# Two half-height products side by side in TensorE's array, in a fused linear-attention and SwiGLU kernel

## The chip, the cores and the metric

The kernel runs on one core of a Trainium2 chip. A core has TensorE (PE; its weight loads are shown as PEld), VectorE (DVE), ScalarE (ACT), GpSimd (POOL) and SyncE (SP, which here issues the DMAs). The metric is the device time of one execution in microseconds (us); lower is better. Of the kernel before there are three timed runs and one profiled execution.

## The reference

For 2048 tokens of 640 features two branches are computed from the same x and mixed by a gate of each token:

```
g   = sigmoid(sum(x * gate_w))
q, k, v = x @ wqkv                       # 32 heads of 20
phi(y)  = concat(softmax(y @ w_phi), softmax(-(y @ w_phi)))
a   = (phi(q) @ (phi(k)^T v)) / (phi(q) . sum(phi(k)) + 1e-6) @ wo
b   = (silu(x @ w_gate) * (x @ w_up)) @ w_down
out = g * a + (1 - g) * b
```

The inner size of the second branch (the feed-forward part) is F = 1728 = 13 x 128 + 64. Inputs and output are bf16.

## The kernel before, in words

Tokens are taken in 16 tiles of 128, or in 4 blocks (`bt`) of 512. Everything that TensorE multiplies lies in SBUF; all products go to PSUM, which is used as 8 banks of 512 f32 columns, or as 4 pairs of banks where a result has 640 columns.

*Feed-forward.* For a block and each of 14 pieces `k` of F (`ffn`, L620), TensorE makes gate and up (5 matmuls of 512 columns each, as 640 = 5 x 128), into one bank each. `ffn_tail` (L592) turns them into a piece of h: ACT takes tanh of the gate into `hT` and copies up into `us`, DVE makes (tanh + 1) * gate in `hT` (L611), POOL multiplies by `us` (L617). Piece 13 has only 64 features: its gate and up stand side by side as one stationary operand of 128 columns (`wg[:, c, 1664:1792]`, L626 to L628), so that gate comes out in PSUM rows 0 to 63 and up in rows 64 to 127. Its h fills rows 0 to 63 of `hT[:, :, 13, :]`; rows 64 to 127 are set to zero once (L543), as are those of `wd[:, 13, :]` (L544).

*Down.* `down` (L709) takes one token tile: 14 matmuls of 512 columns and 14 of 128 into one pair of banks, each with 128 rows (pieces 0 to 12 full, piece 13 half zeros). The stationary operand is a 128x128 tile of `hT`, the moving one a row block of `wd`. The last tile's two column parts are separate tasks, so that the first can be written out while the second runs.

*Attention.* `features` (L799) makes the k and q features: projection on TensorE, then on DVE max, min (L831, L835), two subtractions (L839, L843), exp on ACT, sum and reciprocal on DVE (L854, L858), the division on POOL (L864). `kvpart` sums phi(k)^T v; `qtile` (L922) transposes phi(q) by DMA, multiplies it (`num`), divides, transposes by DMA and multiplies by `wo`. `finish` and `finals` mix the two branches and store a tile.

*What sets the order.* Nothing is ordered by the chip: a planner (`_Plan`, L229) is given every step as a task with an engine, a cost in us, what it depends on, a priority, and what it takes and gives back (a bank, a pair, a slot of a buffer). It plays the program through once by these costs, and each task's instructions are recorded when the planner starts it. So each engine's queue is fixed when the kernel is built, and semaphores guard it when it runs. `down` asks for one pair. The feed-forward and down tasks have priorities by their place in a list (L982 to L993). The constants at L658 to L666 are due times and intervals for k and q tiles (`K_AT`, `K_EACH`, `Q_AT`, `Q_EACH`), and `D_AFTER` and `K_PAIRS` shape the list. All loads (L516 to L535) go through SP's queue in one chain, in which a landing time is assumed for each. All matmuls have one line, that of the helper `mms` (L434), and all activations that of `actop` (L444); they are told apart by their tiles.

Of the kernel before, what the change touches and what calls it, by code (L numbers as in the profile page):

```python
# [6 lines left out]
P = 128  # L7
# [221 lines left out]
class _Plan:  # L229
# [11 lines left out]
    def add(self, eng, cost, fn, deps=(), prio=5.0, lat=None, acq=(), rel=(), name=""):  # L241
        t = _Task(eng, cost, fn, deps, prio, self.LAT[eng] if lat is None else lat,
                  tuple(acq), tuple(rel), len(self.tasks), name)
        self.tasks.append(t)
        return t
# [82 lines left out]
def _mm(*cols):  # L328
    return sum(c / 2400.0 + 0.003 for c in cols)


def _build(
# [22 lines left out]
    def sb(name, shape, dtype):  # L355
        t = nc.alloc_sbuf_tensor(name, list(shape), dtype)
        tr.reg_tensor(t, "sbuf", nc.lookup_mloc(t).addr, rowelems(shape), mybir.dt.size(dtype))
        return t
# [8 lines left out]
    wvg = sb("wvg", [P, 5, D + 1], BF16)  # L367
    wo = sb("wo", [P, 5, D], BF16)
    wd = sb("wd", [P, NK, D], BF16)
    wg = sb("wg", [P, 5, F_FFN + 64], BF16)  # L370
    wu = sb("wu", [P, 5, 13 * P], BF16)
    hT = sb("hT", [P, 2, NK, 512], BF16)
    us = sb("us", [P, 3, 512], BF16)
# [37 lines left out]
    def bank(i, j, c0, c1, r0=0, r1=P):  # L411
        return ps[r0:r1, (2 * i + j) * 512 + c0:(2 * i + j) * 512 + c1]

    def one(b, c0, c1, r0=0, r1=P):
        return ps[r0:r1, b * 512 + c0:b * 512 + c1]
# [22 lines left out]
    def acc(o, pairs):  # L438
        n = len(pairs)
        return [(o, l, r, i == 0, i == n - 1) for i, (l, r) in enumerate(pairs)]  # L440
# [5 lines left out]
    def dveop(fn, reads, writes):  # L446
        run("dve", fn, reads=reads, writes=writes)

    def poolop(fn, reads, writes):
        run("pool", fn, reads=reads, writes=writes)  # L450

    def memset(t_ap, val, eng):
        eobj = {"pool": pool, "dve": dve}[eng]
        run(eng, lambda: eobj.memset(t_ap, val), reads=[], writes=[t_ap])  # L454
# [18 lines left out]
    def load(eng, dst, src, land, prio, transpose=False, name="load", cost=0.06):  # L473

        t = add(eng, cost, lambda: dma(eng, dst, src, transpose=transpose), prio=prio, lat=2.0, name=name)
        t.land = land
        t.slack = L_SLACK if land > 11 else 0.0
        t.after = chain.get(eng)
        chain[eng] = t
        return t  # L480

    def rows(a):
        return a.rearrange("(c p) j -> p c j", p=P)
# [12 lines left out]
    def load_x(bt, prio, *cuts):  # L496

        tok = slice(512 * bt, 512 * bt + 512)
        out_ = []
        for i, (c0, c1, land) in enumerate(cuts):  # L500
            out_ += [load("sp", xT[:, c0:c1, tok], x2[tok, c0 * P:c1 * P], land, prio + 0.1 * i, True, "x%d" % bt)] * (c1 - c0)
        return out_

    def load_wT(which, land, prio):
        o = 5 * which
        return load("sp", wqT[:, o:o + 5, :], A_wqkv[:, which * D:(which + 1) * D], land, prio, True, "wT")
# [3 lines left out]
    def load_gate():  # L510
        with nc.allow_non_contiguous_dma(reason="gate_w column load (640 elems)"):
# [16 lines left out]
    load_gu(4, "sp", (32.4, 33.9), -30)  # L528
    wgl[NPC] = load("sp", wg[:, :, 1664:1728], gsrc[:, :, 1664:1728], 34.2, -29)
    wul[NPC] = load("sp", wg[:, :, 1728:1792], usrc[:, :, 1664:1728], 34.6, -28)  # L530
    xs[3] = load_x(3, -27, (0, 5, 37.4))
    wqT_l = load_wT(0, 41.5, -26)
    wd_l = [load("sp", wd[:, 0:13, :], rows(B_w_down[0:13 * P, :]), 48.5, -25),
            load("sp", wd[0:64, 13, :], B_w_down[13 * P:F_FFN, :], 49.0, -24)]
    wo_l = load("sp", wo[:, :, :], rows(A_wo), 51.0, -23)  # L535
    xl = [x_[4] for x_ in xs]


# [1 line left out]
    zero = add("dve", 0.3, lambda: memset(us[:, 0, :], 0.0, "dve"), prio=-20, name="zero")  # L540
    table = add("act", 1.3, lambda: actop(us[:, 1, 0:1], us[:, 0, 0:1], ACTF.Tanh), deps=[zero], prio=-20, name="table")
    ones_t = add("dve", 0.4, lambda: memset(v1ones, 1.0, "dve"), prio=-19)
    add("dve", 1.0, lambda: memset(hT[64:P, :, 13, :], 0.0, "dve"), prio=-18)  # L543
    wdz = add("dve", 0.7, lambda: memset(wd[64:P, 13, :], 0.0, "dve"), prio=-18)  # L544
    wd_l[1].deps.append(wdz)

    def build_wbd(c):
        nh = PHI_NH[c]
# [42 lines left out]

    def ffn_tail(bt, k, ctx, last, n_after):  # L592
        hb = bt % 2
        rows = P if k < 13 else 64
        hap = hT[0:rows, hb, k, :]

        def gap():
            return one(ctx["g"], 0, 512, 0, rows)

        def uap():  # L600
            return one(ctx["u"], 0, 512) if k < 13 else one(ctx["g"], 0, 512, 64, P)

        def usa():
            return us[0:rows, ctx["us"], :]
        t1 = add("act", 0.49, lambda: actop(hap, gap(), ACTF.Tanh, scale=0.5), deps=[last[0]], prio=0, name="tanh")
        t2 = add("act", 0.49, lambda: actop(usa(), uap(), ACTF.Copy, scale=0.5), deps=[last[1]], prio=0.1,
                 acq=[("us", ctx, "us")], rel=[("bank", ctx, "u")] if k < 13 else (), name="us")

        def stt():
            g_ = gap()  # L610
            dveop(lambda: dve.scalar_tensor_tensor(out=hap, in0=hap, scalar=1.0, in1=g_, op0=ALU.add, op1=ALU.mult),  # L611
                  [hap, g_], [hap])
        t3 = add("dve", 0.59, stt, deps=[t1, t2] if k == 13 else [t1], prio=0, rel=[("bank", ctx, "g")], name="stt")

        def mult():
            u_ = usa()
            poolop(lambda: pool.tensor_tensor(hap, hap, u_, ALU.mult), [hap, u_], [hap])  # L617
        mult_t[bt, k] = add("pool", 1.11, mult, deps=[t2, t3], prio=0, rel=[("us", ctx, "us")], name="hmul")

    def ffn(bt, k, rank):  # L620
        tsl = slice(512 * bt, 512 * bt + 512)
        ctx = {}
        before = [down_t.get((bt - 2, u)) for u in range(4)]
        w_ = w_dep(k)
        if k == 13:
            gu = add("pe", _mm(*[512] * 5), lambda: mms(acc(one(ctx["g"], 0, 512),  # L626
                      [(wg[:, c, 1664:1792], xT[:, c, tsl]) for c in range(5)])),
                      deps=before + [xl[bt], wgl[NPC], wul[NPC]], prio=rank, acq=[("bank", ctx, "g")], name="gu")  # L628
            ffn_tail(bt, k, ctx, (gu, gu), 0)
            return  # L630
        g_ = add("pe", _mm(*[512] * 5), lambda: mms(acc(one(ctx["g"], 0, 512),
                 [(wg[:, c, P * k:P * k + P], xT[:, c, tsl]) for c in range(5)])),
                 deps=before + [xl[bt], wgl[w_]], prio=rank, acq=[("bank", ctx, "g")], name="gate")
        u_ = add("pe", _mm(*[512] * 5), lambda: mms(acc(one(ctx["u"], 0, 512),
                 [(wu[:, c, P * k:P * k + P], xT[:, c, tsl]) for c in range(5)])),
                 deps=[wul[w_]], prio=0.0, acq=[("bank", ctx, "u")], name="up")
        u_.after = g_
        ffn_tail(bt, k, ctx, (g_, u_), 0)
# [17 lines left out]
            ffn_tail(0, k, cs[k], lasts, 0)  # L656

    B_FIRST = 8  # L658
    K_AT, K_EACH, Q_AT, Q_EACH = 26.0, 5.70, 118.6, 8.46
    PRE_Q = 10.10  # L660
    PRE_EACH = 2.2
    PRE_AT = 21.0
    D_AFTER = 1
    FIN_DVE = 12
    K_PAIRS = 7
    store_t = {}  # L666
    gs_t = {}
    pend = []
# [38 lines left out]
                deps=[f], prio=1, name="out")  # L707

    def down(bt, u, rank):  # L709
        t = 4 * bt + u  # L710
        ctx = {}
        hb = bt % 2
        tk = slice(P * u, P * u + P)

        def part(j):
            return acc(bank(ctx["ps"], j, 0, P if j else 512),
                       [(hT[:, hb, k, tk], wd[:, k, 512:D] if j else wd[:, k, 0:512]) for k in range(NK)])
        hold = {"deps": [mult_t[bt, k] for k in range(NK)] + wd_l, "prio": rank, "acq": [("pair", ctx, "ps")], "name": "down"}
        if t < NT - 1:
            d_ = add("pe", _mm(*([512] * 14 + [128] * 14)), lambda: mms(part(0) + part(1)), **hold)  # L720
            down_t[bt, u] = d_
            return t, ctx, d_
        first = add("pe", _mm(*[512] * 14), lambda: mms(part(0)), **hold)
        second = add("pe", _mm(*[128] * 14), lambda: mms(part(1)), prio=0.0, name="down")
        second.after = first
        down_t[bt, u] = second
        return t, ctx, [(first, 0, 512), (second, 512, D)]

# [252 lines left out]
    seq += [("f", k, 0) for k in range(K_PAIRS, NK)]  # L983
    for bt in range(1, NBT):
        ks = list(range(K_PAIRS if bt == 1 else 0, NK))
        ds = [("d", u, bt - 1) for u in range(4)]
        for i, k in enumerate(ks):
            seq.append(("f", k, bt))
            if i >= D_AFTER and ds:
                seq.append(ds.pop(0))  # L990
        seq += ds
    late = [e for e in seq if e[0] == "d" and e[2] == NBT - 2][2:]
    seq = [e for e in seq if e not in late] + late + [("d", u, NBT - 1) for u in range(4)]  # L993
    downs = []
    for i, (kind, j, bt) in enumerate(seq):
        if kind == "f":
            ffn(bt, j, 10.0 + 0.01 * i)
        else:
            downs.append(down(bt, j, 10.0 + 0.01 * i))
    for t in range(NT):  # L1000
        qtile(t, 5.0 + 0.01 * t)
    for t, ctx, d_ in downs:
# [55 lines left out]
```

## Time and profile before

| what | value |
|---|---|
| median of 3 runs (lowest, highest) | 289.60 us (289.57, 289.64) |
| the profiled execution's own time | 289.35 us |
| its span, first to last instruction | 287.2 us |
| granted TensorE clock | 1.000 |
| POOL, division of the features (L864), 32 times | 77.6 us busy |
| TensorE, gate and up matmuls (`wg`, `wu`), 524 records | 131.8 us busy |
| TensorE, down matmuls (`wd`), 443 records | 62.5 us busy |
| DMA, share of 16 engines in the first 40 us | near 1.0 |

A busy time is the time in which at least one instruction of the row or engine ran. The matmul rows need care: TensorE starts a matmul before the one ahead of it has ended, so a mean duration is longer than the distance between starts, and a count times a mean is more than the busy time. A few matmul records are missing (443 of the 448 of `down` are there). "Idle before" is time in which the engine of a row did nothing, with what ended it.

### The profile page before, as it was taken

What the parts mean: (1) busy time and instruction counts of PE and PEld (TensorE: products, weight loads), DVE (VectorE), ACT (ScalarE), POOL (GpSimd) and SP (SyncE); (2) the same over time, 40 slices, a digit from 0 to 9 for tenths busy, and PEclk for the clock granted to TensorE, in tenths of its full rate; (3) what the DMA queues carried; (4) which work ended last, traced back from release to release, by engine and by line L of the source; (5) the groups of instructions that cost most, each with busy time, mean ns of one, the idle gap of its engine ahead of it and who ended that gap; (6) DMA issues with size and microseconds to landing.
All of it is one profiled execution on the core that took longest, in us unless ns stands there. A gap on an engine that the chain in (4) does not pass through costs nothing.

```text
span 287.2 us, 5141 instructions
## 1 busy us (share of the span) xinstructions
PE 281.4 (98%) x2028; PEld 152.0 (53%) x2065; DVE 224.6 (78%) x317; ACT 144.5 (50%) x222; POOL 166.7 (58%) x131
## 2 busy tenths in 40 slices
PE   8999999999999999999999999999999999999996
PEld 2445554555555556555555655554555555555654
DVE  1323498999999998999997779999988897970212
ACT  2546376674865553445445354664664545564110
POOL 5397117677486457565667448688676566655100
PEclk9999999999999999999999999999999999999999
DMA  7999997000000000000234375134444433134211
GB/s 181 237 279 290 244 281 244 1 3 0 2 0 2 0 2 0 2 0 2 50 73 99 61 110 119 40 73 101 80 96 75 96 59 84 29 75 74 71 46 46
DMA packets 65415, 23.90 MB, mean 83 GB/s; under 512 B 53936, under 2 KB 65392, under 8 KB 65392
## 3 DMA queue, kind: packets, MB, share of 16 engines
q1 hardware_dynamic: 64736, 23.58, 36.3%
q8 instruction: 16, 0.26, 0.4%
q10 hardware_dynamic: 656, 0.00, 0.1%
q14 instruction: 7, 0.06, 0.1%
HBM read 8.30 MB, written 2.62 MB: 38 GB/s over the span
## 4 chain that ended last, share of the span: by engine, by line
PE 89%; DVE 9%; issue 1%
PE ps L434 89%; DVE sm L854 2%; DVE hT L611 1%; DVE phi L839 1%; DVE mx L831 1%; DVE mn L835 1%; DVE phi L843 1%; DVE rc L858 1%; DVE kvacc L904 0%; DVE xsb L690 0%; DVE us L454 0%
## 5 line engine op out<-in xcount | busy, mean ns | idle before, releaser
L864 POOL TENSOR_TENSOR phi<-phi,rc 128x1320 bf16<-128x1320 bf16 x32 | 77.6, 2426 | 32.5 <-DVE rc L858 32.5
L617 POOL TENSOR_TENSOR hT<-hT,us 128x512 bf16<-128x512 bf16 (+1 forms) x56 | 64.2, 1154 | 48.8 <-DVE hT L611 29.1
L434 PE MATMUL ps<-xT,wg 128*128 128x512 bf16 x268 | 67.6, 381 | 0.8
L434 PE MATMUL ps<-xT,wu 128*128 128x512 bf16 x256 | 64.2, 379 | 0.2
L434 PE MATMUL ps<-wd,hT 128*128 128x512 bf16 (+1 forms) x443 | 62.5, 298 | 0.3
L854 DVE TENSOR_REDUCE sm<-phi 128x66 f32<-128x1320 bf16 x32 | 48.6, 1518 | 9.5 <-ACT phi L444 9.3
L444 ACT ACTIVATE hT<-ps 128x512 bf16<-128x512 f32 (+1 forms) x56 | 33.2, 594 | 42.1 <-PE ps L434 41.9
L611 DVE SCALAR_TENSOR_TENSOR hT<-hT,ps 128x512 bf16<-128x512 bf16 (+1 forms) x56 | 37.8, 678 | 20.1 <-ACT hT L444 20.0
L444 ACT ACTIVATE phi<-phi 128x1320 bf16<-128x1320 bf16 x32 | 41.6, 1300 | 21.2 <-DVE phi L843 21.2
L434 PEld LDWEIGHTS ps<-wd,hT 128*128 128x128 bf16 x448 | 35.3, 98 | 28.3
L434 PE MATMUL ps<-wqk,xT 128*128 128x512 bf16 (+2 forms) x313 | 47.4, 298 | 0.4
L444 ACT ACTIVATE us<-ps 128x512 bf16<-128x512 f32 (+1 forms) x56 | 33.3, 596 | 17.5 <-PE ps L434 15.8
L434 PEld LDWEIGHTS ps<-xT,wu 128*128 128x128 bf16 x260 | 25.4, 98 | 30.7 <-issue 0.8
L434 PEld LDWEIGHTS ps<-xT,wg 128*128 128x128 bf16 x280 | 25.4, 98 | 24.6 <-issue 1.7
L434 PEld LDWEIGHTS ps<-wqk,xT 128*128 128x128 bf16 x320 | 26.5, 98 | 21.9
L831 DVE TENSOR_REDUCE mx<-ps 128x33 f32<-128x660 f32 x32 | 26.5, 828 | 5.1 <-PE ps L434 5.0
L704 POOL TENSOR_TENSOR xsb<-xsb,xb 128x640 bf16<-128x640 bf16 x12 | 16.8, 1396 | 19.4 <-ACT xb L444 19.4
L843 DVE TENSOR_TENSOR phi<-mn,ps 128x660 bf16<-128x660 f32 x32 | 26.5, 828 | 0.5
L835 DVE TENSOR_REDUCE mn<-ps 128x33 f32<-128x660 f32 x32 | 26.4, 825 | 0.0
L839 DVE TENSOR_TENSOR phi<-ps,mx 128x660 bf16<-128x660 f32 x32 | 26.2, 819 | 0.0
L444 ACT ACTIVATE xsb<-ps,gs 128x640 bf16<-128x640 f32 x16 | 12.6, 789 | 24.4 <-PE ps L434 24.4
L434 PE MATMUL ps<-wo,oT 128*128 128x512 bf16 (+1 forms) x154 | 23.0, 296 | 0.4
(44 smaller groups left out, 183.8 us busy)
## 6 DMA issues: line engine op xcount, KB each, us to landing
out_dram<-xsb SPq DMA_DIRECT2D x15, 160.0 KB, 1.8
wd<-in_B_w_down_dram SPq DMA_DIRECT2D x1, 2080.0 KB, 9.5
wg<-in_B_w_gate_dram SPq DMA_DIRECT2D x3, 320.0 KB, 3.7
wu<-in_B_w_up_dram SPq DMA_DIRECT2D x3, 320.0 KB, 4.3
wvg<-in_A_wqkv_dram SPq DMA_DIRECT2D x1, 800.0 KB, 7.7
wo<-in_A_wo_dram SPq DMA_DIRECT2D x1, 800.0 KB, 10.3
wg<-in_B_w_gate_dram SPq DMA_DIRECT2D x1, 640.0 KB, 4.7
wu<-in_B_w_up_dram SPq DMA_DIRECT2D x1, 640.0 KB, 6.0
```

Source lines behind the costliest of these rows:

```text
L434: last = pe.matmul(o, lhsT=l, rhs=r, start=st, stop=sp_, skip_group_check=True)
L444: run("act", lambda: act.activation(o, i, func, scale=scale), reads=reads, writes=[o])
L611: dveop(lambda: dve.scalar_tensor_tensor(out=hap, in0=hap, scalar=1.0, in1=g_, op0=ALU.add, op1=ALU.mult), [hap, g_], [hap])
L617: poolop(lambda: pool.tensor_tensor(hap, hap, u_, ALU.mult), [hap, u_], [hap])
L704: poolop(lambda: pool.tensor_tensor(x_, x_, b_, ALU.add), [x_, b_], [x_])
L831: dveop(lambda: dve.tensor_reduce(a, b, AX.X, ALU.max), [b], [a])
L835: dveop(lambda: dve.tensor_reduce(a, b, AX.X, ALU.min), [b], [a])
L839: dveop(lambda: dve.tensor_tensor(o_, a, b, ALU.subtract), [a, mx[:, ctx["st"], :]], [o_])
L843: dveop(lambda: dve.tensor_tensor(o_, a, b, ALU.subtract), [b, mn[:, ctx["st"], :]], [o_])
L854: dveop(lambda: dve.tensor_reduce(a, b, AX.X, ALU.add), [b], [a])
L858: dveop(lambda: dve.reciprocal(a, b), [b], [a])
L864: poolop(lambda: pool.tensor_tensor(a, a, b, ALU.mult), [a, r], [a])
```

## The change

Piece 13 is no longer padded. The features 64 to 127 of its rows hold the same 64 features of other tokens: of the four token tiles of a block, tiles 0 and 2 use rows 0 to 63 of `hT[:, hb, 13, 0:256]`, tiles 1 and 3 use rows 64 to 127. For that

- `wg` has 64 more columns, [gate | up | gate], by one more load, and `wd[64:128, 13, :]` holds a second copy of the last 64 rows of w_down, by one more load; the two memsets go.
- piece 13 is made by a new function `edge`: 10 matmuls of 256 columns in place of 5 of 512 (even tiles with [gate | up], odd tiles with [up | gate]), and ACT and DVE operations on 64 rows and 256 columns, two for each one before; POOL has one product of 128 rows and 256 columns.
- `down` takes two tiles at once: first a task `side` with piece 13 of both tiles, four matmuls of 64 rows (512 columns of the first tile, 512 of the second, then 128 of each; the first tile in the lower, the second in the upper rows of the array) that start the sums in two pairs of banks. Then come pieces 0 to 12 of the one tile, then of the other. `side` takes both pairs.
- the planner's due times and the list are changed, the list holds pairs of tiles, and the planner's cost of `side` has a term `SIDES`. Landing times assumed for later loads are 0.4 to 0.9 us later.

```diff
-    wg = sb("wg", [P, 5, F_FFN + 64], BF16)
+    wg = sb("wg", [P, 5, F_FFN + P], BF16)
...
+    wgl2 = load("sp", wg[:, :, 1792:1856], gsrc[:, :, 1664:1728], 35.0, -27.5)
...
+    wd_l += [load("sp", wd[64 * i:64 * i + 64, 13, :], B_w_down[13 * P:F_FFN, :], 49.4 + 0.5 * i, -24.5 + 0.1 * i) for i in range(2)]
...
-    add("dve", 1.0, lambda: memset(hT[64:P, :, 13, :], 0.0, "dve"), prio=-18)
-    wdz = add("dve", 0.7, lambda: memset(wd[64:P, 13, :], 0.0, "dve"), prio=-18)
-    wd_l[1].deps.append(wdz)
...
+    def edge(bt, rank, before):
+        hb = bt % 2
+        ctx = {}
+        hap = hT[:, hb, 13, 0:256]
+        HALF = ((0, 64), (64, P))
+        xv = [xT[:, c, 512 * bt:512 * bt + 512].rearrange("p (a b t) -> p b a t", b=2, t=P) for c in range(5)]
+        def fn():
+            mms([(one(ctx["g"], 256 * j, 256 * j + 256), wg[:, c, 1664 + 64 * j:1792 + 64 * j], xv[c][:, j, :, :], c == 0, c == 4)
+                 for j in range(2) for c in range(5)])
...
+        def tanh():
+            for j, (r0, r1) in enumerate(HALF):
+                actop(hT[r0:r1, hb, 13, 0:256], one(ctx["g"], 256 * j, 256 * j + 256, r0, r1), ACTF.Tanh, scale=0.5)
+        def half_up():
+            for j, (r0, r1) in enumerate(HALF):
+                o0, o1 = HALF[1 - j]
+                actop(us[r0:r1, ctx["us"], 0:256], one(ctx["g"], 256 * j, 256 * j + 256, o0, o1), ACTF.Copy, scale=0.5)
...
-    K_AT, K_EACH, Q_AT, Q_EACH = 26.0, 5.70, 118.6, 8.46
-    PRE_Q = 10.10
+    K_AT, K_EACH, Q_AT, Q_EACH = 24.0, 6.11, 115.0, 8.49
+    PRE_Q = 10.14
...
-    PRE_AT = 21.0
-    D_AFTER = 1
+    PRE_AT = 19.9
+    D_AFTER = 5
...
-    K_PAIRS = 7
+    SIDES = 0.2
+    K_PAIRS = 6
...
     def down(bt, u, rank):
...
+        def sides():
+            mms([(bank(cs[i]["ps"], j, 0, c1 - c0), hT[64 * i:64 * i + 64, hb, 13, 64 * u:64 * u + P], wd[64 * i:64 * i + 64, 13, c0:c1], True, False)
+                 for j, (c0, c1) in enumerate(((0, 512), (512, D))) for i in range(2)])
+        def part(i, j):
+            tk = slice(P * (u + i), P * (u + i) + P)
+            c0, c1 = ((0, 512), (512, D))[j]
+            return [(bank(cs[i]["ps"], j, 0, c1 - c0), hT[:, hb, k, tk], wd[:, k, c0:c1], False, k == 12) for k in range(13)]
+        s_ = add("pe", _mm(512, P) + SIDES, sides, deps=[mult_t[bt, k] for k in range(NK)] + wd_l, prio=rank,
+                 acq=[("pair", cs[0], "ps"), ("pair", cs[1], "ps")], name="side")
```

More of the change, by code (lines that the diff above doesn't have):

```diff
@@ L530, in _build @@
     wul[NPC] = load("sp", wg[:, :, 1728:1792], usrc[:, :, 1664:1728], 34.6, -28)
[L531 to L535, printed above, removed]
+    wgl2 = load("sp", wg[:, :, 1792:1856], gsrc[:, :, 1664:1728], 35.0, -27.5)
+    xs[3] = load_x(3, -27, (0, 5, 37.8))
+    wqT_l = load_wT(0, 41.9, -26)
+    wd_l = [load("sp", wd[:, 0:13, :], rows(B_w_down[0:13 * P, :]), 48.9, -25)]
+    wd_l += [load("sp", wd[64 * i:64 * i + 64, 13, :], B_w_down[13 * P:F_FFN, :], 49.4 + 0.5 * i, -24.5 + 0.1 * i) for i in range(2)]
+    wo_l = load("sp", wo[:, :, :], rows(A_wo), 51.9, -23)
     xl = [x_[4] for x_ in xs]
@@ L593, in ffn_tail @@
         hb = bt % 2
-        rows = P if k < 13 else 64
-        hap = hT[0:rows, hb, k, :]
+        hap = hT[:, hb, k, :]
         def gap():
-            return one(ctx["g"], 0, 512, 0, rows)
+            return one(ctx["g"], 0, 512)
         def uap():
-            return one(ctx["u"], 0, 512) if k < 13 else one(ctx["g"], 0, 512, 64, P)
+            return one(ctx["u"], 0, 512)
         def usa():
-            return us[0:rows, ctx["us"], :]
+            return us[:, ctx["us"], :]
         t1 = add("act", 0.49, lambda: actop(hap, gap(), ACTF.Tanh, scale=0.5), deps=[last[0]], prio=0, name="tanh")
         t2 = add("act", 0.49, lambda: actop(usa(), uap(), ACTF.Copy, scale=0.5), deps=[last[1]], prio=0.1,
-                 acq=[("us", ctx, "us")], rel=[("bank", ctx, "u")] if k < 13 else (), name="us")
+                 acq=[("us", ctx, "us")], rel=[("bank", ctx, "u")], name="us")
         def stt():
@@ L612, in stt @@
                   [hap, g_], [hap])
-        t3 = add("dve", 0.59, stt, deps=[t1, t2] if k == 13 else [t1], prio=0, rel=[("bank", ctx, "g")], name="stt")
+        t3 = add("dve", 0.59, stt, deps=[t1], prio=0, rel=[("bank", ctx, "g")], name="stt")
         def mult():
@@ L618, in ffn_tail, with stt, mult @@
         mult_t[bt, k] = add("pool", 1.11, mult, deps=[t2, t3], prio=0, rel=[("us", ctx, "us")], name="hmul")
+    def edge(bt, rank, before):
[7 more added lines that the diff above has]
+                 for j in range(2) for c in range(5)])
+        gu = add("pe", _mm(*[256] * 10), fn, deps=before + [xl[bt], wgl[NPC], wul[NPC], wgl2], prio=rank,
+                 acq=[("bank", ctx, "g")], name="gu")
+        def tanh():
[5 more added lines that the diff above has]
+                actop(us[r0:r1, ctx["us"], 0:256], one(ctx["g"], 256 * j, 256 * j + 256, o0, o1), ACTF.Copy, scale=0.5)
+        def stt():
+            for j, (r0, r1) in enumerate(HALF):
+                h_ = hT[r0:r1, hb, 13, 0:256]
+                g_ = one(ctx["g"], 256 * j, 256 * j + 256, r0, r1)
+                dveop(lambda h_=h_, g_=g_: dve.scalar_tensor_tensor(out=h_, in0=h_, scalar=1.0, in1=g_, op0=ALU.add, op1=ALU.mult),
+                      [h_, g_, us[:, ctx["us"], 0:256]], [h_])
+        def mult():
+            u_ = us[:, ctx["us"], 0:256]
+            poolop(lambda: pool.tensor_tensor(hap, hap, u_, ALU.mult), [hap, u_], [hap])
+        t1 = add("act", 0.7, tanh, deps=[gu], prio=0, name="tanh")
+        t2 = add("act", 0.7, half_up, deps=[gu], prio=0.1, acq=[("us", ctx, "us")], name="us")
+        t3 = add("dve", 0.7, stt, deps=[t1, t2], prio=0, rel=[("bank", ctx, "g")], name="stt")
+        mult_t[bt, 13] = add("pool", 0.6, mult, deps=[t2, t3], prio=0, rel=[("us", ctx, "us")], name="hmul")
     def ffn(bt, k, rank):
@@ L625, in ffn @@
         if k == 13:
[L626 to L629, printed above, removed]
+            edge(bt, rank, before)
             return
@@ L709, in down @@
     def down(bt, u, rank):
-        t = 4 * bt + u
-        ctx = {}
         hb = bt % 2
[L713 to L727, printed above, removed]
+        cs = ({}, {})
+        last = 4 * bt + u + 1 == NT - 1
+        def sides():
+            mms([(bank(cs[i]["ps"], j, 0, c1 - c0), hT[64 * i:64 * i + 64, hb, 13, 64 * u:64 * u + P], wd[64 * i:64 * i + 64, 13, c0:c1], True, False)
+                 for j, (c0, c1) in enumerate(((0, 512), (512, D))) for i in range(2)])
@@ new lines, in part @@
+        def part(i, j):
[4 more added lines that the diff above has]
+                 acq=[("pair", cs[0], "ps"), ("pair", cs[1], "ps")], name="side")
+        before, out_ = s_, []
+        for i in range(2):
+            pr = 0.0 if i == 0 or last else rank + 0.001
+            if last and i:
+                d1 = add("pe", _mm(*[512] * 13), lambda: mms(part(1, 0)), prio=0.0, name="down")
+                d1.after = before
+                d_ = add("pe", _mm(*[P] * 13), lambda: mms(part(1, 1)), prio=0.0, name="down")
+                d_.after = d1
+                out_.append((4 * bt + u + i, cs[i], [(d1, 0, 512), (d_, 512, D)]))
+            else:
+                d_ = add("pe", _mm(*([512] * 13 + [P] * 13)), lambda i=i: mms(part(i, 0) + part(i, 1)), prio=pr, name="down")
+                d_.after = before
+                out_.append((4 * bt + u + i, cs[i], d_))
+            before = d_
+            down_t[bt, u + i] = d_
@@ L731, in premult @@
+        return out_
     def premult(which, wT_l, prio, step=0.0, at=0.0):
@@ L985, in _build @@
         ks = list(range(K_PAIRS if bt == 1 else 0, NK))
-        ds = [("d", u, bt - 1) for u in range(4)]
+        ds = [("d", u, bt - 1) for u in (0, 2)]
         for i, k in enumerate(ks):
@@ L991, in _build @@
         seq += ds
-    late = [e for e in seq if e[0] == "d" and e[2] == NBT - 2][2:]
-    seq = [e for e in seq if e not in late] + late + [("d", u, NBT - 1) for u in range(4)]
+    late = [e for e in seq if e[0] == "d" and e[2] == NBT - 2][1:]
+    seq = [e for e in seq if e not in late] + late + [("d", u, NBT - 1) for u in (0, 2)]
     downs = []
@@ L998, in _build @@
         else:
-            downs.append(down(bt, j, 10.0 + 0.01 * i))
+            downs += down(bt, j, 10.0 + 0.01 * i)
     for t in range(NT):
```

## The prediction, made before the changed kernel ran

> **What bounds the kernel now.** I read the page's busy line first, then the waits of TensorE alone, then the groups kept apart by shape, then the timeline of the last two tiles. The first fence is from the page's parts 1 and 2, the second the answer on the waits of PE (TensorE's matmul row): who waited for whom, us in total, times, longest.
>
> ```profile
> PE 281.4 (98%) x2028; PEld 152.0 (53%) x2065; DVE 224.6 (78%) x317; ACT 144.5 (50%) x222; POOL 166.7 (58%) x131
> ...
> PEclk9999999999999999999999999999999999999999
> ```
>
> ```profile
> PE ps L434 <- DVE us L454: 1.3, 1, 1.3
> ```
>
> PE is busy for 98% of the span at the full granted clock, and it waited for another engine once: for the first memset, before anything ran. From 1.26 us to the last matmul there is no wait of PE that a faster VectorE (DVE), ScalarE (ACT), GpSimd (POOL) or DMA could shorten. In the middle the chain of waits does pass through DVE for some 27 us, but PE does other work there all the time. So the time is the sum of TensorE's steps: work taken off TensorE is worth its whole step, and work on other engines is worth nothing until it makes TensorE wait.
>
> A step is not the mean of a row. Matmuls overlap, so a row's mean (379 ns) is longer than the distance from one start to the next. The distance comes from runs of matmuls without a gap in the timeline (start, us, engine, line, what, count):
>
> ```profile
> 257.71 1.24 PE L434 MATMUL ps<-xT,wg 128*128 128x512 bf16 x5
> ...
> 277.09 7.77 PE L434 MATMUL ps<-wd,hT 128*128 128x512 bf16 x56
> ```
>
> and from the rows by shape (us busy, mean ns):
>
> ```profile
> L434 PE MATMUL ps<-wd,hT 128*128 128x512 bf16 x219 | 50.4, 379 | 0.3
> L434 PE MATMUL ps<-wd,hT 128*128 128x128 bf16 x224 | 15.1, 219 | 0.0
> ...
> L434 PEld LDWEIGHTS ps<-wd,hT 128*128 128x128 bf16 x448 | 35.3, 98 | 28.3
> ```
>
> Five matmuls of 512 columns take 1.24 us, which is four steps and the last one's 0.379: a step is 0.861 / 4 = 0.215. The 56 of the last two tiles (28 of 512 columns, 28 of 128) take 7.77, less the last one's 0.219, so 7.55 for 28 steps of 512 and 27 of 128: (7.55 - 6.03) / 27 = 0.056. One inner piece k of one token tile in `down` thus costs 0.215 + 0.056 = 0.272 us, whether its 128 rows are full or, as for k = 13, half zeros. The weight loads (PEld, 98 ns each) lie beside matmuls and cost nothing now. The 0.164 us by which 379 ns exceeds the step is the pipe behind a matmul, which the next one covers.
>
> **The change, part by part.**
>
> (1) Removed on TensorE: piece k = 13 of 16 tiles, 16 x 0.272 = 4.35 us. Added: eight groups `side`, each with two matmuls of 512 columns and two of 128, in pairs on the lower and upper 64 rows. If a pair runs at once, a group costs one piece, 0.272, and all eight 2.17. That is a saving of 2.17 us. If the two halves run after each other, a group costs 0.544 and nothing is saved.
>
> (2) `edge`: 20 matmuls of 512 columns (5 in each of 4 blocks) become 40 of 256. On the line through (128, 0.056) and (512, 0.215) a step of 256 is 0.109. 40 x 0.109 - 20 x 0.215 = +0.07 us.
>
> (3) The switch. All matmuls and weight loads of the trace before use 128 rows; none shows what it costs to go from 128-row matmuls to 64-row ones and back, which happens twice in each group, 16 times in all. Call the price s. From below it is 0: the trace steps from 512-column to 128-column matmuls and between operands without loss, and nothing in the sum would make it negative. From above it is the pipe of the last matmul run empty, 0.164, with the next weight load after it uncovered, 0.098: 0.262. The change of time is -2.17 + 0.07 + 16 s = -2.10 + 16 s, between -2.1 and +2.1 us, and zero at s = 0.131. I take 0.098, one whole uncovered weight load and no run-out of the pipe: the new pair of loads goes to half-arrays, and it is the cover of the load that is hardest to keep where the rows change. In the one place in the trace where a load stands uncovered (first line PEld, second PE), the matmul begins 0.03 after the load does, so even this is not a low value:
>
> ```profile
> 5.40 0.14 PEld L434 LDWEIGHTS ps<-xT,wg 128*128 128x128 bf16 x2 [1.02 <-issue]
> ...
> 5.43 1.45 PE L434 MATMUL ps<-xT,wg 128*128 128x512 bf16 x4
> ```
>
> So part (3) costs 16 x 0.098 = 1.57 us.
>
> A rule speaks against the change here. The Trainium skill, page "TensorEngine Tiling (Array Packing)", section "Tiling Modes", says that changing the tiling mode, not merely the tile, drains TensorE. It gives no duration and no run here shows it; it is the second rival below. The skill's page "TensorE: Matmul & The Clock Gate", Part 3, has two tiles in different row groups start about 4 ns apart; by it a group would cost an estimated 8 ns over one piece, 0.06 us in all, which speaks against the third rival.
>
> (4) Other engines. For each block ACT has four activations of 64x256 in place of two of 64x512 (0.59 each), DVE two products in place of one (0.68), POOL one of 256 columns in place of one of 512 (1.15). None is shown at 256 columns; each lies between half and the whole of its row, so ACT gains nothing to 1.2 us a block, DVE nothing to 0.7, POOL -0.6 to 0. What covers this is TensorE's own work: in the order of the changed program between the last `edge` and the first group that reads it stand a group, a `wo`, a `num` and two tiles of `down`, 0.4 + 1.4 + 0.4 + 2 x 13 x 0.272 = 9.2 us of steps, and the tail costs at most 4 x 0.59 + 2 x 0.68 + 1.15 = 4.9. Where that cover fails, the wait would appear at that group. The two memsets that go stand in DVE's first microseconds, where PE does not wait for them: 0. The two added loads (a 64-column slice of the gate weights, 64 rows of `wd`) stand in SP's queue ahead of x of the last block, the two transposed weights and `wo`; like loads landed in
>
> ```profile
> wg<-in_B_w_gate_dram SPq DMA_DIRECT2D x1, 80.0 KB, 5.6
> ...
> wd<-in_B_w_down_dram SPq DMA_DIRECT2D x1, 80.0 KB, 9.3
> ```
>
> and DMA is idle after 50 us, while `down` first reads `wd` at 100 us before and about 107 in the new order: 0, where even 9 us of delay would be covered.
>
> (5) The order. The planner has new due times, so nearly every later row of TensorE moves. Moving work is free so long as nothing waits. Adding steps in both orders, the shortest distance from a q projection to the `num` that needs it falls from 17.7 to 16.2 us, against a chain of 0.83 + 0.83 + 0.82 + 0.83 (DVE) + 1.30 (ACT) + 1.52 + 0.5 (DVE) + 2.43 (POOL) + 3.5 (transposing DMA) = 12.6; that from `num` to its `wo` goes from 6.2 to 6.6. Both keep room: 0. What is new is that a group asks for two free pairs of PSUM banks at once and holds the second one while the first tile's `down` runs.
>
> Sum: -2.17 + 0.07 + 1.57 = -0.5 us. The profiled execution took 289.35 (span 287.2 and 2.15 around it), 0.25 below the median of 289.60; -0.5 gives 288.8 for such an execution and **289.1 us** against the median.
>
> **The rivals.**
>
> A. *The switch is nearly free* (s up to 0.05): -2.1 to -1.3, so 287.5 to 288.3. For it: TensorE loses nothing at any change of shape in the trace. Against: none of those changes the rows.
>
> B. (forecast) s from 0.05 to 0.15: 288.3 to 289.9.
>
> C. *The pipe runs empty at each switch*: s = 0.164 and a load between 0 and 0.098, so +0.5 to +2.1, 290.1 to 291.7. This is the case on the slower side; it decides from s = 0.131. Place: ahead of the first matmul of each `side` and of the first of the `down` behind it. For it: the 0.164 are there in every row, and only the next matmul hides them. Against: all of them would have to be waited for. The drain that the Trainium skill states (part 3) would be this case.
>
> D. *The change doesn't do what it says*: the halves run one after the other. -2.17 falls away; with s = 0.098 that is +1.6, 291.2.
>
> E. *A new wait for banks*: a `side` finds its second pair still held. A pair of a q or k tile is held by four DVE operations, 3.3 us; half of one such hold, 1.7, once, makes it +1.2, 290.8. For it: DVE is busy for 78%, over 95% in parts. Against: before, PE met none in spite of that.
>
> **How the numbers follow.** Chances: A 0.25, B 0.37, C 0.20, D 0.06, E 0.12. A measurement can tell some 0.2%, 0.58 us, from no change. Faster by more: A and the part of B with s below 0.095 (0.17), 0.42. Within: 0.20 of B, 0.03 of C, 0.01 of D, 0.03 of E, 0.27. Slower: 0.17 + 0.05 + 0.09 = 0.31. Cases of both signs hold much of the chance; the likeliest one's own range is 288.3 to 289.9. The range that should hold 8 in 10 goes from A's end, 287.4 (0.1 below 287.5, for the spread of runs), into C, D and E as far as 291.1, which leaves out the upper half of C, D and E, about 0.17.
>
> **What would show it.** In the profile after: wd matmuls of 64 rows, 32 of them, and 416 of 128 rows. From the start of a `side` to the start of its `down`, a piece and one switch, the timeline should show 0.27 to 0.32 (A), 0.32 to 0.42 (B), 0.44 to 0.53 (C), 0.54 and more (D); in D the two halves' starts lie 0.2 apart. The other switch is what the step from the last 128-row matmul to the first of the `side` has over its 0.215 or 0.056. Any line of PE in the waits beside the first one is E. The prediction is wrong in kind if TensorE's steps outside `side` and `edge` change, or if PE waits in more places than one.

## The result, and the profile after

The changed kernel takes **290.41 us** (median of 9 runs, 290.12 to 290.57) against 289.60 of the kernel before (9 runs, 289.27 to 289.89): 0.81 us more, a ratio of 1.0030 with a 95% interval of 1.0022 to 1.0038. Slower by more than 0.2%, where 0.5 us less was forecast; 290.41 lies inside the stated range. The profiled execution took 290.37 us, its span 288.5.

The same rows as before, in the page of the changed kernel:

```profile
PE 284.0 (98%) x2085; PEld 152.3 (53%) x2085; DVE 224.4 (78%) x319; ACT 145.4 (50%) x230; POOL 165.0 (57%) x131
...
PEclk9999999999999999999999999999999999999999
```

TensorE is still what bounds the kernel, at the same clock. The waits of PE (us in total, times, longest) have two new lines, short ones:

```profile
PE ps L434 <- DVE us L454: 1.3, 1, 1.3
PE ps L434 <- ACT us L444: 0.2, 1, 0.2
PE ps L434 <- PE ps L434: 0.2, 1, 0.2
```

The last names TensorE as the one that TensorE waited for. Its full size is not in this list, since a pause after a matmul counts as idle only from that matmul's modelled end. It shows in the groups of the weight loads (PEld; busy, mean ns, then idle before and who ended it), which stand still while TensorE's queue does:

```profile
L434 PE MATMUL ps<-wd,hT 128*128 128x512 bf16 x208 | 47.6, 379 | 0.6 <-PE ps L434 0.2
L434 PEld LDWEIGHTS ps<-wd,hT 128*128 128x128 bf16 x416 | 32.1, 98 | 27.8 <-PE ps L434 2.8 <-issue 0.5
...
L434 PE MATMUL ps<-wd,hT 64*128 64x512 bf16 x16 | 3.1, 387 | 0.0
L434 PE MATMUL ps<-wd,hT 64*128 64x128 bf16 x16 | 1.8, 216 | 0.0
L434 PEld LDWEIGHTS ps<-wd,hT 64*128 64x128 bf16 x32 | 0.9, 94 | 1.3 <-issue 0.6
```

The 32 matmuls of 64 rows are there, and 2.8 us of the loads' idle time ahead of `down` ended with an event of PE itself; before, that row named no releaser. The timeline of the first two groups:

```profile
108.28 0.11 PEld L434 LDWEIGHTS ps<-wd,hT 64*128 64x128 bf16 x4 [0.42 <-issue]
108.29 0.45 PE L434 MATMUL ps<-wd,hT 64*128 64x512 bf16 x4
...
108.86 0.13 PEld L434 LDWEIGHTS ps<-wd,hT 128*128 128x128 bf16 x2 [0.46 <-issue]
```

```profile
123.58 0.11 PEld L434 LDWEIGHTS ps<-wd,hT 64*128 64x128 bf16 x4
124.09 0.98 PEld L434 LDWEIGHTS ps<-wd,hT 128*128 128x128 bf16 x6 [0.40 <-PE ps L434]
```

Two things are read here. The four matmuls of a `side` take 0.45 us to the end of the last one: one step of 512 (0.215), and one matmul of 128 with its end (0.216), and little more. One after the other they would take 0.215 + 0.215 + 0.056 + 0.216 = 0.70. So the halves do run at once; in the trace the second starts 3 to 4 ns after the first. From the first start to the end of the last step a group takes 0.286 us by the starts of its matmuls, 0.014 over a piece. And from the start of the second `side` to the first load of its `down` pass 0.51 us, where the work is 0.27.

The starts of single matmuls give the loss at all eight groups. The first matmul of a `side` starts 0.095 or 0.096 later than the step of the matmul ahead of it, whether that one has 512 columns, 256 or 128. The first matmul of the `down` behind it starts 0.225 later than its step, in the first group 0.315. The other loss is at 86 us: 0.34 between two matmuls, at the kv sums.

```profile
86.62 0.64 PEld L434 LDWEIGHTS ps<-v,phi 128*128 128x128 bf16 x20 [0.35 <-ACT us L444]
```

The kv matmuls need a bank that ACT's copy of an up product sets free, which came late; a shorter gap (0.07) stands at 138 us. The kernel before had neither.

The sum: -2.17 + 0.07 for the work, 8 x 0.096 = 0.77 for the way in, 8 x 0.225 + 0.09 = 1.89 for the way out, 0.41 for the gaps, +0.97; with 8 x 0.014 = 0.11 for the groups, +1.08. The traces agree: from the 46th weight load, which lies behind the start (13.4 us before, 13.6 after), to the end of the last matmul it is 271.44 us before and 272.57 after, +1.13.

The measured time rose by only 0.81 because less of it lies outside the span: 1.90 us in the median of the changed kernel's runs (span 288.5), against 2.15 in 21 runs of the kernel before in the session of e1 (span 287.4). Why it is shorter there is open.

### The profile page after: what moved, and what is told of

Read it like the earlier page. It is cut to its first block, busy times and chain, and to the rows that moved or that the text cites. A ratio compares the mean times of both kernels' runs of the same rounds, so it can differ in the third digit from the quotient of the medians.

```text
span 288.5 us, 5220 instructions
## 1 busy us (share of the span) xinstructions
PE 284.0 (98%) x2085; PEld 152.3 (53%) x2085; DVE 224.4 (78%) x319; ACT 145.4 (50%) x230; POOL 165.0 (57%) x131
## 4 chain that ended last, share of the span: by engine, by line
PE 97%; ACT 1%; DVE 0%; issue 0%
PE ps L434 97%; ACT hT L444 0%; ACT phi L444 0%; DVE xsb L724 0%; ACT us L444 0%; ACT wqk L444 0%; DVE us L454 0%
## 5 line engine op out<-in xcount | busy, mean ns | idle before, releaser
L614 POOL TENSOR_TENSOR hT<-hT,us 128x512 bf16<-128x512 bf16 x52 | 59.5, 1153 | 53.8 <-ACT us L444 25.5
L434 PE MATMUL ps<-xT,wg 128*128 128x512 bf16 (+1 forms) x300 | 69.9, 367 | 0.1
L434 PE MATMUL ps<-wd,hT 128*128 128x512 bf16 (+2 forms) x448 | 62.3, 299 | 0.6 <-PE ps L434 0.2
L444 ACT ACTIVATE hT<-ps 128x512 bf16<-128x512 f32 (+1 forms) x60 | 33.8, 566 | 34.6 <-PE ps L434 34.2
L608 DVE SCALAR_TENSOR_TENSOR hT<-hT,ps 128x512 bf16<-128x512 bf16 x52 | 35.0, 678 | 20.1 <-ACT hT L444 19.9
L434 PE MATMUL ps<-wqk,xT 128*128 128x512 bf16 (+1 forms) x320 | 48.6, 300 | 0.0
L434 PEld LDWEIGHTS ps<-wd,hT 128*128 128x128 bf16 (+1 forms) x448 | 33.0, 97 | 29.1 <-PE ps L434 2.8
L444 ACT ACTIVATE us<-ps 128x512 bf16<-128x512 f32 (+1 forms) x60 | 34.0, 566 | 15.6 <-PE ps L434 13.7
L434 PEld LDWEIGHTS ps<-xT,wg 128*128 128x128 bf16 x300 | 27.7, 98 | 24.4 <-issue 1.7
L434 PE MATMUL ps<-wo,oT 128*128 128x512 bf16 (+1 forms) x160 | 24.3, 299 | 0.0
```

The costliest lines, as they stand in the source:

```text
L434: last = pe.matmul(o, lhsT=l, rhs=r, start=st, stop=sp_, skip_group_check=True)
L444: run("act", lambda: act.activation(o, i, func, scale=scale), reads=reads, writes=[o])
```

## The experiments

The way in costs what the forecast took for a switch. Why does the way out cost more than twice that? **Theory S**: a change of rows costs 0.096 in either direction, and the rest is a wait. `side` and `down` are recorded as two groups, and the recorder makes a group wait for the last event on a bank it writes, also if that is TensorE's own. So the first matmul of `down` waits until the last of `side` has ended and raised its semaphore. **Theory D** (rival C of the prediction): going back to 128 rows needs the pipe run empty, and the semaphore changes nothing. A **third theory, O**, is for the rest: the new order itself brings waits.

**e1: without the wait for TensorE's own semaphore**

```diff
             s, v = ev
+            if s == eng and not own:
+                return
...
-    lambda i=i: mms(part(i, 0) + part(i, 1)), ...
+    lambda i=i: mms(part(i, 0) + part(i, 1), own=i > 0), ...
```

> The changed kernel, with one edit: the first tile's down, which stands right behind its side in TensorE's queue and adds to the banks that side started, no longer waits for the semaphore that side's last matmul raises. Theory S (own semaphore): going back from 64 to 128 rows costs as much as going there, 0.096 us over the step, and the other 0.13 of the 0.226 seen behind each side is TensorE waiting for its own semaphore. Then the gap behind a side falls to about 0.10 over the step, and the time by 8 x 0.13 and 0.09 more in the first group, from 290.4 to 289.3 us. Theory D (drain): the way back is dear in itself, because the pipe runs empty; the gap stays at 0.226 and the time at 290.4.

Measured: 289.29 us (before in the same session 289.57; ratio 0.9992, 0.9983 to 1.0001). The gap behind every `side` is 0.092 or 0.093. The same second group, in the timeline of its weight loads:

```profile
123.56 0.11 PEld L436 LDWEIGHTS ps<-wd,hT 64*128 64x128 bf16 x4
123.94 0.98 PEld L436 LDWEIGHTS ps<-wd,hT 128*128 128x128 bf16 x6 [0.27 <-issue]
```

0.38 us in place of 0.51, and PE is no longer the releaser. That is what theory S said, in the gap and in the time (1.1 us less than the changed kernel). D falls: the change of rows is the same at the same places, and nothing but the wait on the semaphore was removed. The first matmul of `down` now starts 0.067 or 0.068 us before the modelled end of the last one of `side`, so the pipe isn't empty there. From the 46th weight load to the end of the last matmul e1 takes 271.43 us, 1.14 less than the changed kernel.

**e2: the same, with 128 rows in `side`**

```diff
-  hT[64 * i:64 * i + 64, hb, 13, 64 * u:64 * u + P], wd[64 * i:64 * i + 64, 13, c0:c1], True, False)
+  hT[:, hb, 13, 64 * u:64 * u + P], wd[:, 13, c0:c1], True, False)
```

> As e1_no_own_wait, and the four matmuls of side use all 128 rows (so piece 13 of each tile holds the sum of two tiles, which is not what the reference computes). No change of rows and no wait for the own semaphore is left; side costs two pieces, 0.544 us. What is left against the kernel before is the new order and edge. Theory S: 289.6 + 0.07 (edge) + 0.4 (the two short waits of TensorE that the profile after shows at 86 and 138 us) = 290.1; if these waits cost nothing, 289.7. It is slower than e1_no_own_wait by 8 x (0.544 - 0.276 - 0.19) = 0.6. Theory D: it is faster than e1_no_own_wait by 8 x (0.276 + 0.322 - 0.544) = 0.4, about 290.0.

Measured: 289.75 (289.57 before; ratio 1.0005, 0.9996 to 1.0014). It is 0.46 slower than e1: so pairs of half height, with both their switches, do pay, as S has it (0.6), and not as D (0.4 the other way). What the order and `edge` cost without any pair is +0.18 with about 0.26 either way: the 0.48 of the visible gaps and `edge` is just outside, nothing at all is inside. The gaps are there (0.34 at 86.6 us, 0.07 at 138), but how much of them reaches the end is not settled by the time. The traces settle it for these executions: from the 46th weight load to the end of the last matmul e2 takes 271.90 us, 0.46 more than the kernel before, so the gaps and `edge` are there in full.

**e3: the switch alone, in the kernel before**

```diff
-  [(hT[:, hb, k, tk], wd[:, k, 512:D] if j else wd[:, k, 0:512]) for k in range(NK)])
+  [(hT[0:64 if k == 13 else P, hb, k, tk], wd[0:64 if k == 13 else P, k, 512 * j:D if j else 512]) for k in range(NK)])
```

> The kernel before, with one edit: piece 13 in down uses rows 0 to 63 only, one tile at a time, in its old place among the other pieces and in the same accumulation. The columns that TensorE streams are the same; TensorE goes to 64 rows and back twice in each of 16 tiles, 32 times there and 32 times back, and no semaphore stands at any of them. Theory S: 64 x 0.096 = 6.1 us, 295.7. Theory D: 32 x (0.096 + 0.226) = 10.3 us, 299.9. If a change of rows costs nothing by itself: 289.6.

Measured: 296.02 against 289.57, 6.45 us more. Piece 13 of the last tile is TensorE's last work, with no way back behind it, so there are 63 changes and not 64: 0.102 each. Single gaps are 0.095 or 0.096 on the way to 64 rows and 0.102 or 0.103 on the way back, after 512 columns and after 128 alike. The loads show it, around the first one:

```profile
102.66 0.09 PEld L434 LDWEIGHTS ps<-wd,hT 64*128 64x128 bf16 x1 [0.42 <-issue]
102.98 0.39 PEld L434 LDWEIGHTS ps<-wd,hT 128*128 128x128 bf16 x7 [0.23 <-issue]
```

Between them lie 0.32 us, a step of 0.215 and a loss of 0.10. A load whose rows differ from those of the matmul ahead starts late, and its matmul 4 or 5 ns behind it; elsewhere loads run a step ahead. The starts of single matmuls say more: at each of these 63 changes, at the 16 of e1 and at the eight ways in of the changed kernel, the first matmul starts 0.067 or 0.068 us before the modelled end of the matmul ahead. This holds in both directions and for every size, so the pause goes by the end of the matmul ahead and not by the length of the load.

**e4: the own semaphore alone, in the kernel before**

```diff
-  lambda: mms(part(0) + part(1)), **hold)
+  lambda: [mms(part(0)[:7]), mms(part(0)[7:] + part(1))], **hold)
```

> The kernel before, with one edit: down of 15 of the 16 tiles is recorded in two halves, so that after 7 matmuls of 512 columns the eighth, on the same bank, waits for the semaphore that the seventh raises. All matmuls have 128 rows and stand in the old order. Theory S: each such wait lasts until the seventh has ended (0.379 after its start) and some 0.06 for the semaphore, 0.44 in place of a step of 0.215, so 15 x 0.23 = 3.4 us, 293.0. Theory D: a wait for TensorE's own semaphore on an order that holds anyway costs nothing, 289.6.

Measured: 293.26 against 289.57, 3.69 us for 15 waits, 0.246 each; single gaps 0.223 or 0.224, and 0.27 to 0.31 in three places where another wait comes with it. In the timeline of the loads, with no row changed anywhere:

```profile
107.25 1.39 PEld L434 LDWEIGHTS ps<-wd,hT 128*128 128x128 bf16 x7
109.20 0.33 PEld L434 LDWEIGHTS ps<-wd,hT 128*128 128x128 bf16 x3 [0.55 <-PE ps L434]
```

So a wait of TensorE for itself costs as much as the way out of `side`, with the same releaser, and covers the change of rows there: 0.225 with both, 0.092 with the change alone (e1), 0.223 with the wait alone.

**e5 and e6: the order.** e5 gives the planner the durations of `edge` that the profile shows; e6 puts back the old due times.

```diff
-  t1 = add("act", 0.7, tanh, deps=[gu], prio=0, name="tanh")
+  t1 = add("act", 0.82, tanh, deps=[gu], prio=0, name="tanh")
...
-  t3 = add("dve", 0.7, stt, deps=[t1, t2], ...)
+  t3 = add("dve", 0.84, stt, deps=[t1, t2], ...)
...
```

```diff
-    K_AT, K_EACH, Q_AT, Q_EACH = 24.0, 6.11, 115.0, 8.49
+    K_AT, K_EACH, Q_AT, Q_EACH = 26.0, 5.70, 118.6, 8.46
...
-    D_AFTER = 5
+    D_AFTER = 1
...
```

> As e1_no_own_wait, with the planner's costs of edge set to what the profile after shows (ACT 0.82 in place of 0.7 for each pair of activations, DVE 0.84 for 0.7, POOL 0.66 for 0.6), which moves the order of the work. Theory O: the wait of TensorE for 0.34 us at 86 us is there because ACT's work after the first edge is planned too short, so that a bank comes free later than planned; with the right costs the planner puts other work there, and the time falls from 289.3 to 288.9, 0.6 under the kernel before. Rival: the wait has to do with other costs or other waits come in its place, 289.3 or more.

> As e1_no_own_wait, with the due times, D_AFTER and K_PAIRS of the kernel before. TensorE's own steps are those of e1_no_own_wait: 2.10 less than before and 16 x 0.096 = 1.54 more for the changes of rows, -0.56. If the order brings no wait of TensorE: 289.0. If side, which asks for two pairs of banks, finds one of them held under the old times: above 289.3, with lines of PE in the waits.

Measured: 290.16 (e5; ratio 1.0016, 1.0007 to 1.0026) and 293.77 (e6; 1.0149, 1.0122 to 1.0175), each against 289.66. In e5 the gap at 86 us is gone while TensorE's order is that of e1 up to 152 us. Behind that the order moved and other waits came; the expected gain did not. The waits of PE of e5:

```profile
PE ps L436 <- ACT xsb L446: 0.8, 1, 0.8
...
PE ps L436 <- DMA oT<-ob: 0.2, 1, 0.2
```

and of e6:

```profile
PE ps L436 <- DVE hT L647: 1.7, 1, 1.7
...
PE ps L436 <- DVE hT L610: 1.1, 2, 0.7
```

L647 is DVE's product in `edge`, which sets the bank of an `edge` free. A `side` of the other block stands 1.4 us behind that `edge` in TensorE's queue and waits for the bank, 1.9 us in one place: rival E, under the old times. The new constants belong to the change; without them it is 4 us slower than the kernel before, even with the own wait taken out.

**e7 and e9: no wait for TensorE's own semaphore anywhere**, in the changed kernel (`own=False` in every call) and in the kernel before (the same return in the recorder, for PE).

> As e1_no_own_wait, and no matmul anywhere waits for TensorE's own semaphore. Elsewhere such a wait is for matmuls that ended long before, so theory S expects next to nothing: 289.2 to 289.3, at most 0.07 less for the place at 138 us, where the wait stands in an instruction of its own. If own waits cost something wherever they stand, as there are over a hundred: under 288.9.

> The kernel before, with no matmul waiting for TensorE's own semaphore. Its profile shows no wait of that kind that lasts, so theory S expects 289.5 to 289.6, no difference that a measurement can tell. If it is faster by 0.3 us, the gain of e1 and e7 over the kernel before is that of the waits in general and not of the 64-row pairs.

Measured: e7 289.38 (against 289.66; ratio 0.9990, 0.9981 to 0.9999), e9 289.61 (against 289.68; 0.9996, 0.9987 to 1.0005). So own waits cost something that these times can tell only where the event is fresh, as behind `side` and in e4.

**e8 and e10: the gap at 86 us.** A group of kv matmuls is moved behind the next task in TensorE's queue by holding its recording back: the second such group in e8 (shown), the fourth in e10.

```diff
...
+  if t.name == "kv" and self.kv_n == 2 and self.late is None:
+      self.late = t.fn
+  else:
+      t.fn()
+      if e == "pe" and callable(self.late):
+          self.late()
+          self.late = False
```

> As e7_no_own_waits_at_all, with two neighbours changed over in TensorE's queue and nothing moved on any other engine: the second half of the first block's kv sums, which waited 0.34 us for ACT at 86 us, comes behind the 0.4 us of premultiplications that stood after it. Theory O: this wait is time lost to the new order; filled with work that was to be done anyway, it gives back up to 0.34 us, 289.0 in place of 289.4 and 0.6 under the kernel before. Rival: the wait only moves to the next instruction, 289.4.

> As e7_no_own_waits_at_all, with the right neighbours changed over (e8 moved the kv sums of block 0, and the wait belongs to those of block 1): the second half of the kv sums of block 1 comes behind the five gate matmuls (1.08 us) that stood after it; nothing moves on another engine. Theory O: the 0.34 us at 86 us go, 289.0 in place of 289.3, some 0.6 under the kernel before. Rival: the gate matmuls wait as well, or what comes after them does, 289.3.

Measured: e8 289.28 (against 289.68; 0.9989, 0.9980 to 0.9998), and the gap at 86 us stands as it was: I had moved the kv sums of the wrong block, so e8 says nothing of theory O and is a second e7. e10 289.67 (against 289.69; 1.0002, 0.9993 to 1.0011): the gate matmuls in the place of the kv sums wait too, now for DVE, and longer:

```profile
PE ps L446 <- DVE kvacc L966: 0.4, 1, 0.4
```

So the rival of e10 holds: two independent groups wait at this place, and changing over neighbours does not remove it. What would, without new waits elsewhere, is open.

## Why the prediction was wrong, step by step

- *What bounds the kernel*: right for the span: every difference found in it is a step or a pause of TensorE. The clock row it leaned on does not show the half-speed steps of the first 6 to 7 us (last section); they are in both kernels.
- *Part (1)*: right. The pairs run at once; -2.17 us is there but for 0.11. The Trainium skill's page "TensorE: Matmul & The Clock Gate", Part 3, has tiles in different row groups start about 4 ns apart; this trace has 3 to 4 ns. A whole group costs 14 ns over a piece.
- *Part (2)*: right. Ten matmuls of 256 columns in the profile after:

```profile
258.81 1.26 PE L434 MATMUL ps<-xT,wg 128*128 128x256 bf16 x10
```

(1.26 - 0.272) / 9 = 0.110 a step, against 0.109.
- *Part (3), the switch*: right in size, by luck. I took 0.098; it is 0.095 to 0.096 there and 0.092 to 0.103 back. The choice between the ends was a guess, and its reason, a weight load left uncovered, is not what the traces show: the matmul starts 4 or 5 ns after its load, so the load's time runs beside it, and the loss lies ahead of the load. It goes by the end of the matmul ahead, as in rival C, but with 0.096 of the 0.164 of pipe on the way in (0.164 - 0.068). The Trainium skill's page "TensorEngine Tiling (Array Packing)", section "Tiling Modes", says that a change of mode drains TensorE. The pause agrees with that as far as it goes by the end of the matmul ahead; the next matmul still starts 0.068 before that end, and what it waits for no run shows.
- *The step that failed* is the sum's silence between parts (1) and (3): I counted the matmuls of `side` and `down` and the switches between them, and took it that TensorE goes from one to the other without a wait. The change cuts one group in two on the same bank, and the recorder makes a wait out of every such cut. That is 8 x 0.13 + 0.09 = 1.1 us, and e1 gives it back (290.41 to 289.29). The miss was 1.3 us (290.41 against 289.1). With this wait out of the way the forecast is off by 0.2, and that is partly luck: the sum had neither the 0.41 of gaps (part 5) nor the 0.11 of the groups, and in e1 some 0.3 less outside the span stands against them (1.84 us, before 2.15).
- *My own mark misled.* From a `side` to its `down` the prediction set 0.44 to 0.53 as the sign of rival C. It was 0.51, and C was wrong: a wait for a matmul's end and a pipe that runs empty look the same in that number. The releaser in the weight loads' row told them apart, and e1 showed it.
- *Part (4)*: the sizes were in their bounds (ACT 0.378 for a 64x256 activation, DVE 0.417, POOL 0.668), and `side` did not wait for `edge`.
- *Part (5)*: wrong in part. I looked at two distances and gave the order 0; the trace shows 0.41 us of gaps at places I had not looked at. Rival E, a `side` that waits for banks, does not occur under the new times (under the old ones it does, e6); the gap at 86 us has its form, but belongs to the kv sums and is a fifth of its size.

What is left is small. The medians of e1, e7 and e8 are 0.28 to 0.40 us under the kernel before, 0.1%, at the edge of what can be told (e7 and e8 exclude 1, e1 just not). But the median spans of the same runs differ by 0.1 at most, in both directions: 287.5, 287.4 and 287.4 us against 287.4, 287.5 and 287.5. Most of the gain lies outside the span, 1.84 to 2.01 us against 2.15 to 2.18, where no matmul stands, and no run shows its cause. On TensorE the pairs give -2.17 + 0.11 + 0.07 + 16 x 0.094 = -0.5 us, as the 0.46 between e1 and e2 bears out, and the 0.41 of new gaps take nearly all of it.

## What to carry to other kernels

When a change cuts an accumulation into two recorded groups, look for the semaphore that joins them: here TensorE, made to wait for its own last matmul, paid that matmul's whole end, 0.22 us each, though the order held anyway. Half-height pairs save a full step only once per group, and each group pays two changes of rows, here 0.19 us of the 0.27 saved; so groups should be few and long, which no run here tried. On an engine with no slack, a new order is a cost of its own until its profile shows no new gaps.

## What was not expected of the hardware

- A change between 128 and 64 rows costs 0.092 to 0.103 us, after 128, 256 and 512 columns alike. The next matmul starts 0.067 or 0.068 us before the modelled end of the one ahead, and its weight load, which elsewhere starts a step earlier, 4 or 5 ns before it (e1, e3).
- A wait on TensorE's own semaphore costs 0.223 us in a run of 512-column matmuls: 0.164 to the matmul's end and 0.06 from there to the next start. A second wait at the same place adds some 0.04 to 0.09 (three places in e4; behind the first `side` of the changed kernel, where the wait is an instruction of its own, 0.09).
- At the start TensorE runs at half speed while the page's clock row shows 9. In e10's profiled execution x landed 0.7 us late, and the slow stretch went on to 10 us:

```profile
5.99 1.86 PE L446 MATMUL ps<-xT,wg 128*128 128x512 bf16 x4 [0.71 <-DMA xT<-in_A_x_dram]
7.64 1.91 PE L446 MATMUL ps<-xT,wu 128*128 128x512 bf16 x4
9.35 1.41 PE L446 MATMUL ps<-xT,wg 128*128 128x512 bf16 x4
```

(1.91 - 0.63) / 3 = 0.427 a step, twice 0.215, where 0.63 is the time of one such matmul. That execution took 291.32 us against a median of 289.67, so a single execution, the profiled one included, can stand over a microsecond from the median for a reason in its first 10 us.
